# Pooled outputs of two batches issued by two engines, and a list scheduler that is told how long issuing a transfer takes

## The chip, the cores and the metric

The kernel runs on one core of one Trainium2 chip. The metric is the device time of one execution in microseconds (us). The kernel before has a median of 968.46 us over 3 runs (966.66 to 969.57).

The engines have these names here: TensorE (PE in the profile; its weight loads are PEld), VectorE (DVE), ScalarE (ACT), GpSimd (POOL) and SyncE (SP; SPq is its queue, which issues transfers). Each engine works through its own queue in order. An instruction that waits holds back all that stands behind it on the same engine.

## The reference

Attention with a pooled and a local part, followed by a token and channel mixer, for 8 batches of 8 heads, 576 positions and a head dimension of 64, all in float32:

```python
q_d, k_d, v_d = (means over 4 neighbouring positions: 144 positions)
out_d     = softmax(q_d @ k_d.T / 8) @ v_d
out_up    = np.repeat(out_d, 4, axis=2)
mask      = np.abs(pos[:, None] - pos[None, :]) < 4
out_local = softmax(where(mask, q @ k.T / 8, -1e9)) @ v
x  = (out_up + out_local), heads side by side: (8, 576, 512)
h  = relu(x^T @ w_tok1) @ w_tok2          # tokens 576 -> 256 -> 576
u  = x + h^T
h2 = relu(u @ w_ch1) @ w_ch2              # channels 512 -> 1536 -> 512
result = u + h2
```

## The kernel before

**Work of one batch.** Queries and keys arrive as four tiles `qk`, values twice: as `vr` (rearranged for pooling) and as `vw` (windows of rows for the local part). `pool_q` and `load_v` sum groups of four positions; for batch 0 the queries and keys are summed on VectorE, otherwise GpSimd does it. `pooled(st, two)` computes the pooled attention of one half of the heads: scores `sd`, exponentials `pd`, their transposes `td`, products `ad` with the pooled values `vd`, and the normalized output `od`. After the second half, the twelve blocks of `od` are copied by twelve transfers of 24 KB into the last rows of each window of `vw`. So the local part can add the pooled output: `local(st, t)` takes one of five tiles of positions, computes local scores `sc`, probabilities `P`, their transposes `pT`, and multiplies them with `vw` (`av`, line 576). The eight rows of `vw` that the pooled output fills are multiplied by a fixed pattern of ones, and the sum of both outputs comes from the same product. Its result is copied to `x` by ScalarE (line 581).

**Mixer.** `mix` splits `x` into two parts (`xh`), multiplies with W1 (`t`, then `hid`) and W2, adds `x`, and scales the result to two float16 parts (`uh`). `first` and `second` are the channel products (`c`, in two chunks of 256 and 320 positions, three float16 passes each); each of the twelve output tiles of `first` is split again by ScalarE and VectorE (`h`, lines 761 and 763).

**Weights.** They come as raw 64-bit words and are turned into float32 in the kernel: `to_f32` uses ScalarE (line 217), GpSimd (220, 223) and VectorE (228). W has nine pieces (five raw buffers), C1 and C2 have twelve tiles each (six raw buffers for C1; the raw tiles of C2 go into the buffers of `qk` and `vw` of batch 0, once these are read). All of this takes place beside batch 0.

**Order of the work.** The order of instructions on each engine is fixed when the program is built. For the start (batch 0 with all weights, and most of batch 1's attention and mixer) `drive` does it: a list scheduler over 71 streams, which are generators that yield steps. A step has an engine, a planned time, what it needs, and PSUM or SBUF slots that it takes and gives. `drive` takes the step that can start first by its own clocks; among steps of the same engine that could start within 0.15 us (`PATIENCE`) it takes the one whose stream stands first in `ORDER`:

```python
t = max([clock[e], it[2] if at is None else at] + [made[n] for n in needs] + ...)
...
best = min(some, key=lambda x: x[0])
best = max((x for x in some if x[0] <= best[0] + PATIENCE and x[1][1][0] == best[1][1][0]),
           key=lambda x: x[1][3])
```

Engine letters in steps are A ScalarE, G GpSimd, V VectorE, P TensorE, S SyncE. The streams are L (loads: 0 pooling of `qk`, 1 `vr`, 2 W, 3 `vw`, 4 C1, 5 C2), A and a (attention of batch 0 and 1: 0 and 1 pooled, 2 to 6 the local tiles), M and m (mixer of batch 0 and 1), U (what follows the channel products), W (conversion of W), S (scale of C1), C and D (conversion of C1 and C2), T (C2's second step), H and h (loads of batches 1 and 2), P and Q (channel products of batch 0). Where TensorE would wait before batch 0's first channel products, `keep_busy` puts products of a constant tile in (`busy`, line 157). What is left over when batch 0 is done, and batches 2 to 7, is woven between the channel products by a fixed rule that does not use `ORDER`.

The transfers of the pooled output and the planned time at which the windows are complete (`full`):

```python
yield step("S", 0.2, ("vw", b), ("od", b, 0), at=e)
for c, k, s, odd, par, jq in blocks():
    nc.sync.dma_start(st.vw[...], st.od[...])
make(("full", b), e, 3.0)
```

Of the kernel before, what the change touches and what calls it, by code (L numbers as in the profile page):

```python
# [20 lines left out]
WB = QB + 6  # L21
KB = 1 + WB + QB // 4
# [10 lines left out]
PATIENCE = 0.15  # L33


ORDER = ("P0 L2 T0 W0 D7 m1 L1 m0 C11 D11 C7 U1 P1 L5 W6 W5 W7 D5 L4 D2 C0 C6 C1 U0 A4 h0 C4 W3 M3 m3 D4 L3 M2 "
         "U2 A6 D10 S0 D9 a6 a0 C5 L0 A3 A2 M0 a1 C8 A1 D0 m2 a3 A5 W1 H0 M1 a5 W4 Q0 W8 D6 D8 a2 A0 D1 C9 W2 "
         "C2 C10 D3 C3 a4 ").split()


@with_exitstack
def tile_ups_attention_mixer(ctx, tc, qk, vw, vr, w1, w2, c1, c2, out):
# [87 lines left out]

    clock = dict(A=2.0, G=5.0, V=2.0, P=0.0, S=0.0, D=0.0)
    now = [0.0]
    free = {k: {i: 0.0 for i in range(n)} for k, n in SLOTS.items()}
    held = {}
# [2 lines left out]
    def step(engine, us, *needs, at=None, take="", give=""):  # L139
        return engine, us, needs, at, take.split(), give.split()  # L140

    def make(what, t, late=0.0):
        made[what] = (t or 0.0) + late
# [87 lines left out]
    def weight_loads(pieces, tag, name):  # L231
        raws = {}
        for i, (src, n) in enumerate(pieces):
            yield step("S", 0.1, *([(name, "read", i - BUFS[tag])] if i >= BUFS[tag] else []))
            raws[i] = T([src.shape[0], 2 * n], U32, tag, f"{name}{i}_raw")
            nc.sync.dma_start(raws[i], src)
            made[name, "raw", i] = fetched(src.shape[0] * n * 8)
            made[name, "raw"] = raws
# [87 lines left out]
    class Second(Channel):  # L326
# [22 lines left out]
        def loads(self):  # L349

            self.raws = made["C2", "raw"] = []
            for i in range(NF):
                if i < 4:
                    yield step("S", 0.1, *(("tile", 0, t) for t in range(len(TILES))))
                    t = T([128, S + KW], F32, "qk", f"C2_raw{i}")[:, :1024].bitcast(U32)
                else:
                    if i == 4:
                        yield step("S", 0.1, *(("av", 0, t) for t in range(len(TILES))))
                        four = T([128, 4, 1024], U32, "vw", "C2_raws")
                    elif i >= 8:  # L360
                        yield step("S", 0.1, ("C2", "read", i - 4))
                    t = four[:, i % 4]
                nc.sync.dma_start(t, u32(c2[i]))
                self.raws.append(t)
                made["C2", "raw", i] = fetched(2 ** 19)
# [28 lines left out]
    def load_v(st):  # L394
        st.vd = T([128, 3, 4, D + 1], F32, "vd", f"vd{st.b}")
        nc.gpsimd.memset(st.vd[:, :, :, D:D + 1], 4.0)
        ts, arrives = {}, {}

        def fetch(i):
            two, kc = divmod(i, 3)  # L400

            tag = "w" if st.b > 1 else "x" if st.b or i < BUFS["x"] else "xh"
            ts[i] = T([128, 4, 128], F32, tag, f"vr{st.b}_{i}")
            nc.sync.dma_start(ts[i], vr[st.b, kc, two].rearrange("p (r c) -> p r c", r=4))
            arrives[i] = fetched(262e3)

        early = {0: 6, 1: 5}.get(st.b, 0)
        if early:
            yield step("S", 0.1, *([("mixed", 0)] if st.b else []))
        for i in range(early):  # L410
            fetch(i)
        for i in range(6):
            two, kc = divmod(i, 3)
            if i >= early:
                fetch(i)
            t = ts.pop(i)
            e = yield step("G", 1.25, at=arrives[i])
            nc.gpsimd.tensor_add(t[:, 0:2], t[:, 0:2], t[:, 2:4])  # L418
            nc.gpsimd.tensor_add(st.vd[:, kc, 2 * two:2 * two + 2, :D], t[:, 0].rearrange("p (h d) -> p h d", d=D),
                                 t[:, 1].rearrange("p (h d) -> p h d", d=D))  # L420
            make(("v", st.b, i), e)
# [43 lines left out]
    def pooled(st, two):  # L465

        b = st.b
        yield step("P", 0.9, ("q", b, 2 * two + 1), take="gg")
        ps = P2(f"sd{b}_{two}")
        for c, k, s, odd, par, jq in blocks():  # L470
            x = st.qd[64 * par:64 * par + 64, 2 * two + odd]
            nc.tensor.matmul(ps[64 * c:64 * c + 64, k, Sd * s:Sd * s + Sd], x[:, QC * jq:QC * jq + 64], x[:, Sd:],  # L472
                             start=True, stop=True)
        mx = T([128, 2, 3], F32, "sm", f"mxd{b}_{two}")
        nm = T([128, 2, 3], F32, "nm", f"nmd{b}_{two}")
        s_ = ps[:, :, :3 * Sd].rearrange("p a (s w) -> p a s w", s=3)
        yield step("V", 1.25)
        nc.vector.tensor_reduce(mx, s_, axis=AX.X, op=ALU.max)
        nc.vector.tensor_scalar(nm, mx, -0.125 / 16, None, ALU.mult)
        yield step("A", 2.1, take="w", give="gg")  # L480
        pd = T([128, 2, 3, Sd], F32, "w", f"pd{b}_{two}")
        for k in range(2):
            for s in range(3):
                nc.scalar.activation(pd[:, k, s], s_[:, k, s], AF.Exp, bias=nm[:, k, s:s + 1], scale=0.125 / 16)  # L484
        yield step("P", 1.1, take="gg", give="w")
        ps = P2(f"td{b}_{two}")
        flat = pd.rearrange("p k s w -> p (k s w)")
        for kc in range(3):
            for c, k, s, _, par, _ in blocks():
                o, i = Sd * kc + QC * s, Sd * (3 * k + s) + QC * kc  # L490
                for i, n in [(i, 64)] if i + 64 <= 6 * Sd else [(i - 16, 64), (i, QC)]:
                    nc.tensor.matmul(ps[64 * par:64 * par + n, k, o:o + QC], flat[64 * c:64 * c + QC, i:i + n],  # L492
                                     ident[64 * c:64 * c + QC, 64 * c:64 * c + QC], start=True, stop=True)
        yield step("A", 0.95, take="w", give="gg")
        pt = T([128, 2, 3 * Sd], F32, "w", f"ptd{b}_{two}")
        nc.scalar.copy(pt[:64 + QC], ps[:64 + QC, :, :3 * Sd])
        yield step("P", 1.1, ("v", b, 3 * two + 2), take="gg", give="w")
        ps = P2(f"ad{b}_{two}")
        flat = pt.rearrange("p k n -> p (k n)")
        for t in range(3):  # L500
            for kc in range(3):
                for c, k, s, odd, par, _ in blocks():
                    if s == t:
                        o = 3 * Sd * k + Sd * kc + QC * s
                        n = min(64, 6 * Sd - o)
                        p = slice(64 * par, 64 * par + QC)
                        nc.tensor.matmul(ps[64 * c:64 * c + n, k, (D + 1) * s:(D + 1) * s + D + 1], flat[p, o:o + n],  # L507
                                         st.vd[p, kc, 2 * two + odd], start=kc == 0, stop=kc == 2)
        if not hasattr(st, "od"):
            st.od = T([128, 2, 3, 2, D], F32, "od", f"od{b}")  # L510
        ps = ps[:, :, :3 * (D + 1)].rearrange("p k (s w) -> p k s w", s=3)
        r = T([128, 2, 3], F32, "sm", f"rd{b}_{two}")
        e = yield step("V", 0.8, give="gg")
        nc.vector.tensor_scalar(r, ps[:, :, :, D], 4 * EPS, None, ALU.add)
        nc.vector.reciprocal(r, r)
        nc.vector.tensor_tensor(st.od[:, :, :, two], ps[:, :, :, :D], r.unsqueeze(3).to_broadcast([128, 2, 3, D]),
                                ALU.mult)
        make(("od", b, two), e)
        if two == 1:
            yield step("S", 0.2, ("vw", b), ("od", b, 0), at=e)  # L520
            for c, k, s, odd, par, jq in blocks():
                nc.sync.dma_start(st.vw[64 * par + 1 + WB:64 * par + KB, CG * jq:CG * jq + CG, 128 * odd:128 * odd + 128],  # L522
                                  st.od[64 * c:64 * c + QC, k, s].rearrange("p a d -> p (a d)"))
            make(("full", b), e, 3.0)
        make(("pair", b, two), e)

    def local(st, t):
# [38 lines left out]
        yield step("A", 0.59, give=one)  # L566
        nc.scalar.copy(pt, ps[:, :4 * n].rearrange("p (hp s) -> p hp s", hp=4))
        make(("tile", b, t), e)
        e = yield step("P", 0.8, ("full", b), ("vw", b), take="gg")
        ps = P2(f"av{b}_{t}")  # L570
        for hp in range(4):
            for j in range(nb):
# [144 lines left out]

    def ahead(b):

        yield step("S", 0.1, *([("C2", "read", i) for i in range(4)] + [("pair", 0, 1)] if b == 1 else []))  # L720
        st = load(b)
        if b > 1:
            load_w(st)
        yield from pool_all(st)
        yield from load_v(st)
        if b == 1:
            yield step("S", 0.1, *(("C2", "read", i) for i in range(4, NF)))
            load_w(st)

    def side(b):  # L730
# [94 lines left out]
        return mixes[b]  # L825

    def windows(st):
        yield step("S", 0.1)
        load_w(st)

    last = len(TILES) - 1
# [135 lines left out]
```

## Time and profile before

| what | value |
|---|---|
| median of 3 runs | 968.46 us (966.66 to 969.57) |
| the profiled execution | 967.55 us, of it 965.7 us from first to last instruction |
| mean TensorE clock granted | 0.975 |
| busy: TensorE, VectorE, ScalarE, GpSimd | 908.6, 431.0, 302.9, 202.6 us |
| constant products that keep TensorE busy (first 200 us) | 75, 24.8 us |
| moved by DMA | 71.67 MB |

Rows of a timeline give start and length in us, engine, line, operation, output from inputs, how many were merged; in brackets the idle time of that engine just before and what ended it. The forty digits of a slice row are busy tenths of 24 us each. In rows of stretches each engine's busy time is followed by its number of instructions. A row of the chain has start, length and the work that the end of the program was waiting for then.

### The profile page before, as it was taken

Reading aid. Unit: us, or ns where it says so; the run is one execution under the profiler, and the core shown is the slowest. Engines: PE = TensorE matmul, PEld = TensorE weight load, DVE = VectorE, ACT = ScalarE, POOL = GpSimd, SP = SyncE. Lnnn points to the kernel's source line nnn. Section 1 sums busy time; section 2 is a strip of 40 time slices with the busy share of each in tenths; the row PEclk is TensorE's granted clock in tenths of the full one; section 3 lists DMA queues with packets and bytes.
Section 4 is the critical chain, followed back from the end, with each engine's and each line's share of the span. In section 5 each row is a group of like instructions: output and inputs, shape, how many; then the busy total and the mean of one; then the engine's idle time right before and its main releaser. Section 6 shows DMA issues by size and latency. Waiting matters only on the chain.

```text
span 965.7 us, 29151 instructions
## 1 busy us (share of the span) xinstructions
PE 908.6 (94%) x13143; PEld 696.8 (72%) x13143; DVE 431.0 (45%) x982; ACT 302.9 (31%) x675; POOL 202.6 (21%) x301
## 2 busy tenths in 40 slices
PE   7658798999999999999999999999999999999998
PEld 3446576877867787777877787777777778777875
DVE  7539984526353354334353344324443254333221
ACT  2346463314242143223232142322332142322110
POOL 5659950042231002300122002300113000000000
PEclk8779799999999999999999999999999999999999
DMA  9561630251242012600243002500234000000000
GB/s 341 133 241 60 239 74 14 88 138 52 64 160 39 22 33 68 170 8 22 59 147 59 14 27 80 171 1 28 53 95 117 7 23 21 18 1 28 12 12 28
DMA packets 31756, 71.67 MB, mean 74 GB/s; under 512 B 3808, under 2 KB 16608, under 8 KB 31008
## 3 DMA queue, kind: packets, MB, share of 16 engines
q1 hardware_dynamic: 31632, 69.81, 24.0%
q8 instruction: 103, 1.69, 0.7%
q14 instruction: 21, 0.17, 0.1%
HBM read 58.00 MB, written 9.44 MB: 70 GB/s over the span
## 4 chain that ended last, share of the span: by engine, by line
PE 79%; DVE 10%; ACT 4%; issue 3%; SPq 1%; DMA 1%; POOL 0%; ACTq 0%; DVEq 0%
PE c L120 53%; PE t L120 11%; PE av L576 3%; PE ad L507 2%; PE td L492 2%; PE t L640 2%; PE pT L563 2%; PE sc L540 2%; DVE uh L686 1%; ACT pd L484 1%; SPq L522 1%; PE sd L472 1%; DVE P L552 1%; DVE r L557 1%; DVE mx L551 1%
## 5 line engine op out<-in xcount | busy, mean ns | idle before, releaser
L120 PE MATMUL c<-uh,CW 128*128 128x256 f16 (+1 forms) x2304 | 307.9, 288 | 0.4 <-DVE uh L686 0.4
L120 PE MATMUL c<-h,CX 128*128 128x256 f16 (+1 forms) x2304 | 306.2, 286 | 0.0
L120 PEld LDWEIGHTS <-CW 128*128 128x128 f16 x2304 | 218.2, 98 | 68.1 <-issue 12.2
L120 PEld LDWEIGHTS <-CX 128*128 128x128 f16 x2304 | 216.0, 98 | 60.6 <-issue 1.5
L763 DVE SCALAR_TENSOR_TENSOR h<-c,h 128x256 f16<-128x256 f32 (+1 forms) x192 | 87.7, 457 | 190.6 <-ACT h L761 190.4
L761 ACT ACTIVATE h<-c 128x256 f16<-128x256 f32 (+1 forms) x192 | 78.7, 410 | 237.9 <-PE c L120 237.6
L418 POOL TENSOR_TENSOR vr<-vr 128x256 f32<-128x256 f32 x48 | 36.9, 769 | 372.9 <-DMA vr<-in_vr_dram 350.2
L789 DVE SCALAR_TENSOR_TENSOR u<-c,io,u 128x256 f32<-128x256 f32 (+1 forms) x64 | 32.9, 514 | 104.3 <-PE c L120 104.2
L120 PE MATMUL t<-xh,W 128*128 128x512 f32 (+1 forms) x240 | 67.7, 418 | 0.3 <-ACT x L581 0.2
L120 PE MATMUL t<-W,hid 128*128 128x256 f32 (+1 forms) x384 | 66.9, 309 | 0.0
L443 POOL TENSOR_TENSOR qs<-qk 128x288 f32<-128x288 f32 x56 | 39.8, 711 | 125.5 <-DMA qk<-in_qk_dram 65.7
L665 ACT COPY u<-t 128x256 f32<-128x256 f32 (+1 forms) x64 | 25.4, 397 | 118.2 <-PE t L120 100.5
L667 DVE TENSOR_REDUCE umx<-t 128x1 f32<-128x256 f32 (+1 forms) x64 | 29.2, 456 | 67.0 <-ACT u L665 67.0
L618 DVE TENSOR_TENSOR xh<-x,xh 128x512 fp32r<-128x512 f32 (+1 forms) x40 | 30.9, 774 | 57.8 <-ACT xh L616 57.8
L576 PE MATMUL av<-vw,pt 47*32 47x64 f32 x2304 | 40.6, 230 | 15.6 <-DMA vw<-od 10.7
L120 PEld LDWEIGHTS t<-W,hid 128*128 128x128 f32 x384 | 53.0, 188 | 2.2
L120 PEld LDWEIGHTS t<-xh,W 128*128 128x128 f32 (+1 forms) x240 | 43.6, 193 | 11.4 <-issue 2.2
L576 PEld LDWEIGHTS av<-vw,pt 47*32 47x32 f32 x2304 | 29.3, 108 | 28.6 <-DMA vw<-od 12.6
L581 ACT COPY x<-av 128x512 f32<-128x512 f32 (+1 forms) x40 | 23.3, 583 | 68.3 <-PE av L576 59.9
L554 ACT ACTIVATE P<-P 128x304 f32<-128x304 f32 (+1 forms) x40 | 18.4, 459 | 67.8 <-DVE P L552 67.4
L684 ACT ACTIVATE uh<-u,us 128x256 f16<-128x256 f32 (+1 forms) x64 | 29.8, 524 | 28.4 <-DVE us L126 18.1
L686 DVE SCALAR_TENSOR_TENSOR uh<-u,us,uh 128x256 f16<-128x256 f32 (+1 forms) x64 | 34.0, 575 | 5.1 <-ACT uh L684 5.0
(107 smaller groups left out, 844.6 us busy)
## 6 DMA issues: line engine op xcount, KB each, us to landing
qk<-in_qk_dram SPq DMA_DIRECT2D x32, 579.0 KB
vr<-in_vr_dram SPq DMA_DIRECT2D x48, 256.0 KB
vw<-in_vw_dram SPq DMA_DIRECT2D x16, 702.0 KB
C_raw<-in_c_dram SPq DMA_DIRECT2D x16, 512.0 KB
out_dram<-u SPq DMA_DIRECT2D x32, 160.0 KB
C_raws<-in_c_dram SPq DMA_DIRECT2D x8, 512.0 KB
out_dram<-u SPq DMA_DIRECT2D x32, 128.0 KB
vw<-od SPq DMA_DIRECT2D x96, 24.0 KB
```

Of the source, the lines that this page charges most:

```text
L120: nc.tensor.matmul(ps, lhs(a), rhs(c), start=first and i == 0, stop=last and i == 2, **kw)
L418: nc.gpsimd.tensor_add(t[:, 0:2], t[:, 0:2], t[:, 2:4])
L443: nc.gpsimd.tensor_add(two, x[:, :, 0:2], x[:, :, 2:4])
L576: nc.tensor.matmul(ps[QB * j:QB * j + QB, par, D * hp:D * hp + D], pt[p, hp, QB * j:QB * j + QB], st.vw[p, g, D * COLUMN[hp]:D * COLUMN[hp ...
L618: nc.vector.tensor_tensor(xh[:, 1], xf(t), xh[:, 0].bitcast(F32), ALU.subtract)
L665: nc.scalar.copy(u, ps)
L667: nc.vector.tensor_reduce(umx[ch][:, c:c + 1], ps, axis=AX.X, op=ALU.max, apply_absolute_value=True)
L684: nc.scalar.activation(t[:, 0], st.u[ch][c], AF.Copy, scale=s)
L686: nc.vector.scalar_tensor_tensor(t[:, 1], st.u[ch][c], s, t[:, 0], ALU.mult, ALU.subtract)
L761: nc.scalar.activation(ht[:, 0], ps, AF.Relu)
L763: nc.vector.scalar_tensor_tensor(ht[:, 1], ps, 0.0, ht[:, 0], ALU.max, ALU.subtract)
L789: nc.vector.scalar_tensor_tensor(us[c], banks[c], io, us[c], ALU.mult, ALU.add)
```

## The change

The twelve transfers of the pooled output become two steps in batches 0 and 1: four are issued by ScalarE (planned 2.72 us) and eight by SyncE (planned 5.44 us), both at the time the output is ready; the windows are planned complete 2.0 us after SyncE's step instead of 3.0 us after the output. Other batches keep twelve on SyncE. Issuing a load is planned at 0.65 us instead of 0.1, each load of `vr` and of C2 has a step of its own, and SyncE's planned clock starts at 3.0. Some planned times of TensorE's steps grow (pooled attention from 0.9, 1.1, 1.1 to 1.1 in batches 0 and 1, 1.3, 1.3; the local products of batch 0 from 0.8 to 1.2). `ORDER` is a new permutation of the same 71 names. No arithmetic, tile or transfer is added or removed.

```diff
-ORDER = ("P0 L2 T0 W0 D7 m1 L1 m0 C11 D11 C7 U1 P1 L5 W6 W5 W7 D5 L4 D2 C0 C6 C1 U0 A4 h0 C4 W3 M3 m3 D4 L3 M2 "
-         "U2 A6 D10 S0 D9 a6 a0 C5 L0 A3 A2 M0 a1 C8 A1 D0 m2 a3 A5 W1 H0 M1 a5 W4 Q0 W8 D6 D8 a2 A0 D1 C9 W2 "
-         "C2 C10 D3 C3 a4 ").split()
+ORDER = ("h0 D4 M1 W6 U0 T0 D10 P1 C6 M3 C2 W5 C4 D2 D5 M2 W0 L2 m0 D11 C7 L0 a0 W4 S0 C10 D6 L5 m1 W3 W1 D7 "
+         "L1 a5 C5 A0 M0 A6 C8 A2 U2 A4 A1 L4 C1 C3 P0 C9 U1 m3 C11 m2 a6 W2 A5 a1 a4 D8 A3 D0 Q0 D1 H0 a3 W7 "
+         "D3 D9 W8 a2 L3 C0 ").split()
+ISSUE = 0.65
...
-    clock = dict(A=2.0, G=5.0, V=2.0, P=0.0, S=0.0, D=0.0)
+    clock = dict(A=2.0, G=5.0, V=2.0, P=0.0, S=3.0, D=0.0)
...  (weight_loads)
-            yield step("S", 0.1, *([(name, "read", i - BUFS[tag])] if i >= BUFS[tag] else []))
+            yield step("S", ISSUE, *([(name, "read", i - BUFS[tag])] if i >= BUFS[tag] else []))
...  (C2.loads)
                 if i < 4:
-                    yield step("S", 0.1, *(("tile", 0, t) for t in range(len(TILES))))
+                    yield step("S", ISSUE, *(("tile", 0, t) for t in range(len(TILES))))
                     t = T([128, S + KW], F32, "qk", f"C2_raw{i}")[:, :1024].bitcast(U32)
                 else:
+                    yield step("S", ISSUE, *((("av", 0, t) for t in range(len(TILES))) if i < 8 else [("C2", "read", i - 4)]))
                     if i == 4:
-                        yield step("S", 0.1, *(("av", 0, t) for t in range(len(TILES))))
                         four = T([128, 4, 1024], U32, "vw", "C2_raws")
-                    elif i >= 8:
-                        yield step("S", 0.1, ("C2", "read", i - 4))
...  (load_v)
-        if early:
-            yield step("S", 0.1, *([("mixed", 0)] if st.b else []))
         for i in range(early):
+            yield step("S", ISSUE, *([("mixed", 0)] if st.b and i == 0 else []))
             fetch(i)
...  (pooled)
-        yield step("P", 0.9, ("q", b, 2 * two + 1), take="gg")
+        yield step("P", 0.9 if b > 1 else 1.1, ("q", b, 2 * two + 1), take="gg")
...
-        yield step("P", 1.1, take="gg", give="w")
+        yield step("P", 1.3, take="gg", give="w")
...
-        yield step("P", 1.1, ("v", b, 3 * two + 2), take="gg", give="w")
+        yield step("P", 1.3, ("v", b, 3 * two + 2), take="gg", give="w")
...
         if two == 1:
-            yield step("S", 0.2, ("vw", b), ("od", b, 0), at=e)
-            for c, k, s, odd, par, jq in blocks():
-                nc.sync.dma_start(st.vw[...], st.od[...])
-            make(("full", b), e, 3.0)
+            ready_at = e
+            for engine, share in ((("A", (0, 4)), ("S", (4, 12))) if b < 2 else (("S", (0, 12)),)):
+                e = yield step(engine, 0.68 * (share[1] - share[0]) if b < 2 else 0.2, ("vw", b), ("od", b, 0), at=ready_at)
+                for c, k, s, odd, par, jq in list(blocks())[share[0]:share[1]]:
+                    rows = st.vw[...]
+                    (nc.scalar if engine == "A" else nc.sync).dma_start(rows, st.od[...])
+            make(("full", b), e, 2.0 if b < 2 else 3.0)
...  (local)
-        e = yield step("P", 0.8, ("full", b), ("vw", b), take="gg")
+        e = yield step("P", 0.8 if b else 1.2, ("full", b), ("vw", b), take="gg")
...  (ahead, windows)
-        yield step("S", 0.1, *([("C2", "read", i) for i in range(4)] + [("pair", 0, 1)] if b == 1 else []))
+        yield step("S", 4 * ISSUE if b == 1 else 0.1, *([("C2", "read", i) for i in range(4)] + [("pair", 0, 1)] if b == 1 else []))
...
-            yield step("S", 0.1, *(("C2", "read", i) for i in range(4, NF)))
+            yield step("S", 2 * ISSUE, *(("C2", "read", i) for i in range(4, NF)))
...
-        yield step("S", 0.1)
+        yield step("S", 2 * ISSUE)
```

More of the change, by code (lines that the diff above doesn't have):

```diff
@@ L519, in pooled @@
         if two == 1:
-            yield step("S", 0.2, ("vw", b), ("od", b, 0), at=e)
-            for c, k, s, odd, par, jq in blocks():
-                nc.sync.dma_start(st.vw[64 * par + 1 + WB:64 * par + KB, CG * jq:CG * jq + CG, 128 * odd:128 * odd + 128],
-                                  st.od[64 * c:64 * c + QC, k, s].rearrange("p a d -> p (a d)"))
-            make(("full", b), e, 3.0)
+            ready_at = e
+            for engine, share in ((("A", (0, 4)), ("S", (4, 12))) if b < 2 else (("S", (0, 12)),)):
+                e = yield step(engine, 0.68 * (share[1] - share[0]) if b < 2 else 0.2, ("vw", b), ("od", b, 0), at=ready_at)
+                for c, k, s, odd, par, jq in list(blocks())[share[0]:share[1]]:
+                    rows = st.vw[64 * par + 1 + WB:64 * par + KB, CG * jq:CG * jq + CG, 128 * odd:128 * odd + 128]
+                    (nc.scalar if engine == "A" else nc.sync).dma_start(rows, st.od[64 * c:64 * c + QC, k, s].rearrange("p a d -> p (a d)"))
+            make(("full", b), e, 2.0 if b < 2 else 3.0)
         make(("pair", b, two), e)
```

## The prediction

> **What bounds the kernel now.** I read the page first: the span, the forty slices, the DMA queues.
>
> ```profile
> span 965.7 us, 29151 instructions
> PE   7658798999999999999999999999999999999998
> DVE  7539984526353354334353344324443254333221
> POOL 5659950042231002300122002300113000000000
> PEclk8779799999999999999999999999999999999999
> DMA  9561630251242012600243002500234000000000
> q8 instruction: 103, 1.69, 0.7%
> ```
>
> The reader is to see two kernels in one. From slice 10 (about 240 us) on, TensorE is at 9 in nearly every slice at full clock. Before that it has holes, its clock drops, and VectorE and GpSimd stand at 9 in slices 3 and 4. The table of importance and the changed costs mostly work in that first part, so I cut the span into five stretches, and two of them finer:
>
> ```profile
> core 0: us, PE busy (x) PEld busy (x) DVE busy (x) ACT busy (x) POOL busy (x), PEclk, DMA share, GB/s
> 0.00:110.00 110.00, 76.31 (x1194) 49.69 (x1195) 76.92 (x155) 46.24 (x98) 77.54 (x94) 0.82 0.57 188
> 110.00:150.00 40.00, 40.00 (x610) 32.04 (x610) 31.93 (x71) 23.08 (x51) 23.76 (x34) 0.95 0.48 140
> 150.00:170.00 20.00, 16.37 (x259) 11.49 (x256) 9.68 (x21) 6.89 (x14) 0.00 (x0) 0.91 0.07 16
> 170.00:240.00 70.00, 67.75 (x970) 53.24 (x969) 32.56 (x73) 21.89 (x52) 17.23 (x29) 1.00 0.33 96
> 240.00:965.70 725.70, 708.19 (x10119) 550.33 (x10116) 279.89 (x664) 204.80 (x463) 84.03 (x145) 1.00 0.18 53
> 41.00:58.00 17.00, 9.95 (x243) 6.14 (x235) 4.83 (x12) 2.14 (x5) 0.18 (x1) 0.70 0.20 53
> 60.00:118.00 58.00, 43.68 (x410) 31.81 (x408) 50.50 (x87) 32.27 (x63) 53.70 (x48) 0.85 0.52 192
> ```
>
> Columns: length, then busy time of TensorE, weight load, VectorE, ScalarE, GpSimd, clock, DMA share. TensorE lacks 110.00 - 76.31 = 33.69 us in the first 110 us, nothing to 150, 20.00 - 16.37 = 3.63 around 160, 70.00 - 67.75 = 2.25 to 240. After 240 it is 708.19 / 725.70 = 98% busy with work that the change does not touch; whatever is won or lost before simply shifts it. From 60 to 118 us GpSimd is busy 53.70 of 58.00 us and VectorE 50.50: this stretch is paced by converting the weights. But from 41 to 58 us GpSimd works 0.18 of 17.00 us and VectorE 4.83. That hole is where the change acts; the timelines of the engines and the chain show what fills it:
>
> ```profile
> 46.36 0.56 DVE L516 TENSOR_TENSOR od<-ad,rd 128x384 f32<-128x384 f32 x1
> 46.95 8.67 SPq L522 DMA_DIRECT2D vw<-od  x12
> 54.24 2.17 DMA vw<-od
> 54.31 0.44 PE L576 MATMUL av<-vw,pt 47*32 47x64 f32 x8 [2.56 <-DMA vw<-od]
> 56.45 1.75 PE L576 MATMUL av<-vw,pt 47*32 47x64 f32 x102 [1.01 <-DMA vw<-od]
> 42.76 0.74 ACT L246 CAST W<-W_raw 128x256 fp32r<-128x256 f32 x2
> 57.37 0.59 ACT L581 COPY x<-av 128x512 f32<-128x512 f32 x1 [13.88 <-PE av L576]
> 57.85 0.67 ACT L217 ACTIVATE C_raw<-C_raw 128x512 f32<-128x512 f32 x1
> 58.68 1.35 POOL L223 TENSOR_SCALAR C_raw<-C_raw 128x512 bf16<-128x512 f32 x1 [17.50 <-ACT C_raw L217]
> 55.66 1.49 SPq L236 DMA_DIRECT2D W_raw<-in_w_dram  x2
> ```
>
> The pooled output of batch 0 is written at 46.36 + 0.56 = 46.92. SyncE then issues its twelve transfers one after another for 8.67 us, the last lands 2.17 us after its issue began, and the local `av` products, which read these rows, run in drips until 56.45. ScalarE's next instruction is the copy of `x` (13.88 us waiting on `av`), and behind it in its queue stands the conversion of a C1 tile, for which GpSimd waits 17.50 us. Two more weight loads stand on SyncE behind the twelve. One issue train thus stops five engines. Batch 1 repeats it with TensorE better covered:
>
> ```profile
> 152.60 8.56 SPq L522 DMA_DIRECT2D vw<-od  x12
> 159.85 0.32 PE L576 MATMUL av<-vw,pt 47*32 47x64 f32 x8 [2.10 <-DMA vw<-od]
> 160.57 0.30 PE L576 MATMUL av<-vw,pt 47*32 47x64 f32 x2 [0.41 <-DMA vw<-od]
> 161.98 0.76 PE L576 MATMUL av<-vw,pt 47*32 47x64 f32 x38 [1.11 <-DMA vw<-od]
> 162.68 3.21 PE L120 MATMUL c<-uh,CW 128*128 128x320 f16 x12
> 167.03 1.79 PE L120 MATMUL c<-uh,CW 128*128 128x320 f16 x12
> ```
>
> 8.56 us of issues, and TensorE idle 2.10 + 0.41 + 1.11 = 3.62 us of the 3.63 that the stretch lacks.
>
> **The change part by part.** Durations are from the profiled execution, 967.55 us (span 965.7 and 1.85 around it); the median of the runs shown is 968.46, 0.91 above it.
>
> *The split, batch 0.* No transfer is added; four of twelve move from SyncE to ScalarE, in the first two batches only.
>
> ```profile
> L522 SPq DMA_DIRECT2D vw<-od x96: 668/669/1573, 46.9 to 812.9; - x96
> ```
>
> One issue is 0.669 us, 8.67 / 12 = 0.72 with the gap. Eight in a row end the train four issues sooner: 4 x 0.72 = 2.9 us, the four of ScalarE running beside them. I take -2.9. Bounds: 0, if ScalarE comes to its four so late that its last lands no sooner than now, and -2.9, since SyncE still has eight. What queues behind them: SyncE's weight loads (at 55.66) move up as much; on ScalarE four issues cost 4 x 0.669 = 2.7 us (no row shows ScalarE issuing; I use SyncE's median, its ends 0.668 and 1.573 give 2.7 to 6.3), which lie in a stretch where ScalarE is busy 2.14 of 17 us. The DMA engines are nearly empty there, share 0.20 in the stretch from 41 to 58. [...]
>
> *The new costs around the store, batch 0.* The planner had the pooled rows ready 3.0 us after the output is written; the profile has 56.45 - 46.92 = 9.5 us. After the change it plans 8 x 0.68 + 2.0 = 7.44 us against 8 x 0.72 + 2.17 = 7.9 us to expect. It sees 7.44 - 3.0 = 4.4 us more of wait, and fills queues with what can start earlier: the C1 conversion at 57.85 should stand ahead of the copy at 57.37 and GpSimd resume sooner. The lower bound is 0 (nothing is moved ahead, or the copy stays first); the upper is the idle 17.50 us less the 2.9 already counted, 14.6, because GpSimd at 53.70 of 58.00 passes an earlier start on nearly whole. I take half of the 4.4, -2.2, nearer the lower end, since VectorE paces the same stretch and its chain begins with that `x`, which does not move by this.
>
> *The split, batch 1.* SyncE's train from 152.60 ends four issues sooner, 4 x 8.56 / 12 = 2.9 us of the 3.62 idle. There is a second term: right after the wait, twelve 128x320 matmuls take 3.21 us where the same twelve take 1.79 at 167.03, and the stretch's clock is 0.91. With some 0.8 us of idle left I expect full clock, 1.4 us more. The nearest row that a shorter wait keeps the clock is the stretch from 170 to 240: 2.25 us idle in pieces, clock 1.00. [...] Sum -4.3, bounds 0 and -(3.6 + 1.4) = -5.0 as gain; as loss ScalarE's 2.7 us of issuing stand in front of `h` and `CX` work, of which SyncE's place shows nothing: at most +2.7 if the products wait for it. ScalarE is idle half of that time, so I add 0.
>
> *Separate steps for transfers, 0.65 us each, and SyncE's clock starting at 3.0.* No instruction is added. The six `vr` loads, now one block, will interleave with weight loads:
>
> ```profile
> 3.44 4.95 SPq L404 DMA_DIRECT2D vr<-in_vr_dram  x6
> 21.84 0.64 POOL L419 TENSOR_TENSOR vd<-vr 128x128 f32<-128x128 f32 x1
> 30.49 0.33 PE L507 MATMUL ad<-vd,ptd 48*64 48x65 f32 x4 [0.66 <-ACT ptd L496]
> 36.41 2.22 PE L507 MATMUL ad<-vd,ptd 48*64 48x65 f32 x68 [5.59 <-issue]
> 32.66 0.66 ACT L217 ACTIVATE C_raw<-C_raw 128x512 f32<-128x512 f32 x1
> 34.00:36.00 2.00, 0.00 (x0) 0.00 (x0) 0.00 (x0) 0.00 (x0) 1.84 (x3) 0.50 0.87 323
> ```
>
> The last `vr` is issued by 3.44 + 4.95 = 8.4 us. With up to eight loads between the six, at the 0.72 us of the train above, it is some 5 us later. Its sum on GpSimd ends at 22.5 now and its first user is at 30.49: 8 us of cover, cost 0; without the cover at most 5 us, and the gain of weights that come sooner at most the same. The sixth to eighth C2 load become steps of their own, and the loads of batch 1 (2.6 us where it was 0.1) and of `vw` (1.3) are costed: the order on SyncE may change, no transfer is added, and what they feed (C2, batch 1) is read tens of microseconds later, cost 0.
>
> *Larger costs of pooled products and first `av`; the new table.* Only the order of each engine's queue changes. The table decides among steps of one engine that can start within 0.15 us, so nearly always where an engine is behind. What that is worth no row shows. Bounds by the nearest: the 5.59 us gap at 36.41 (TensorE waits for nothing shown, VectorE and ScalarE run dry behind it) may vanish or come twice, so -5.6 to +5.6. I take 0.
>
> Sum: -2.9 - 2.2 - 4.3 = -9.4, so 967.55 - 9.4 = 958.2, and 0.9 up for the median: 959.1 us.
>
> **The rivals.** *Conversions refill the hole.* If the planner puts two thirds of the 17.50 us of GpSimd's idle to use, 11.7 + 4.3 = 16.0 us go: 952.5. For it: GpSimd at 93% afterwards. Against: VectorE at 87% and products waiting for `x`.
>
> *ScalarE is held, slower.* ScalarE's four issues wait in its queue for the pooled output. Its last conversion before that ends at 43.50, 3.4 us ahead of the output. If the new order puts the issues ahead of conversions and something like the 5.59 us gap delays the output, GpSimd starves behind ScalarE as it now does behind `x`, but earlier, and batch 1's `h` can be caught the same way. Each microsecond goes to the end at 93%; from 9.4 + 2.9 = 12.3 us of extra hold it decides. Measured from the last ScalarE work before the gap, 32.66 + 0.66 = 33.3, to 46.92 the hold is 13.6 us: 968.46 - 9.4 + 13.6 = 972.7.
>
> *The gain is given back.* Batch 1's own chain ends just in time now:
>
> ```profile
> 228.48 0.38 PE L120 MATMUL c<-uh,CW 128*128 128x256 f16 x2 [0.41 <-DVE uh L686]
> 231.88 2.08 DVE uh L686 x3
> ```
>
> TensorE goes from the last products of batch 0 to the first of batch 1 with 0.41 us idle, the scaled inputs (`uh`) finished as they are read. If batch 0 ends 9 us sooner and the chain of batch 1 does not (its tiles `a1`, `a2`, `a3` fall from places 46, 62, 51 to 56, 69, 64 of 71), TensorE waits there and 7 to 9.4 us of the gain return: 966 to 968.5, middle 967. Against it: TensorE is full from 110 to 150, so batch 1's steps wait for TensorE and move with it. A code-loading wait would act alike: the page's instruction row has 103 transfers, and the 5.59 us gap, in which nothing but GpSimd works, falls where the DMA engines are busy at 0.87; one more such gap takes 5.6 of the 9.4 (964.7, still the forecast), two take it all.
>
> **How the numbers follow.** 0.3%, about what a measurement here can tell from no change, is 2.9 us: 965.6 to 971.4. Forecast (953 to 965) 0.50; refill 0.14; given back 0.17; held 0.19. The first two are faster, 0.64; the third the same, 0.17; the last slower, 0.19. The range for eight in ten takes the first three, from 948 (batch 0 at 14.6 + 2.9 and batch 1 at 4.3 would be 946.7; most of it is enough) to 972.
>
> **What would show it.** Right: SyncE with eight transfers in about 5.7 us after the output of batch 0 and four on ScalarE beside them; `av` finished starting about 7.9 us after the output; GpSimd's idle of 17.50 us cut to 12 or less; the wait before `av` of batch 1 under 1 us and no twelve at 3.21 us; the same 725 us from the place that is now 240 on. Wrong: ScalarE's issues late or ahead of conversions that GpSimd waits for; a new idle piece of TensorE over 3 us at the change from batch 0 to 1; the 5.59 us gap larger or doubled.

## The result, and the profile after

The changed kernel takes 956.8 us in the median of 4 runs (950.54 to 957.6); the kernel before, beside it, 967.56 us (965.69 to 969.57). The ratio is 0.9874, 95% interval 0.9827 to 0.9922: 10.8 us, or 1.3%, faster. A second series gave 0.9878 (0.9851 to 0.9904). The profiled execution took 957.6 us, its span is 955.6.

The page of the changed kernel:

```profile
span 955.6 us, 29167 instructions
PE   7568999999999999999999999999999999999998
PEclk8877799999999999999999999999999999999999
q10 hardware_dynamic: 448, 0.20, 0.1%
```

q10, ScalarE's transfer queue, is new: 448 packets, 0.20 MB, the stores that moved. TensorE still has its holes in the first slices and is at 9 after that. The stretches (length, then busy time of TensorE, weight load, VectorE, ScalarE, GpSimd, clock, DMA share):

```profile
0.00:110.00 110.00, 80.70 (x1194) 51.61 (x1195) 77.27 (x161) 47.25 (x99) 78.43 (x95) 0.77 0.58 190
110.00:150.00 40.00, 40.00 (x556) 32.03 (x554) 30.41 (x66) 22.82 (x52) 23.66 (x33) 0.98 0.45 135
150.00:170.00 20.00, 20.00 (x496) 16.21 (x494) 13.07 (x32) 6.29 (x12) 0.00 (x0) 1.00 0.11 30
170.00:240.00 70.00, 68.10 (x985) 53.59 (x983) 30.70 (x68) 24.48 (x57) 17.12 (x30) 1.00 0.32 96
```

TensorE is busy for 20.00 of 20.00 us from 150 to 170, where it had been for 16.37: the wait in batch 1 is gone, and the clock there is 1.00 instead of 0.91. Until 110 us it is busy 4.4 us longer, but the clock is 0.77 instead of 0.82. To place the gain I cut each span at two events: TensorE's first channel product of batch 0 ("first c") and of batch 1 ("seam"). Of the kernel before, then of the changed one:

```profile
110.37 2.76 PE L120 MATMUL c<-uh,CW 128*128 128x256 f16 x12
226.81 1.26 PE L120 MATMUL c<-uh,CW 128*128 128x256 f16 x10
```

```profile
108.57 2.77 PE L121 MATMUL c<-uh,CW 128*128 128x256 f16 x12
219.28 1.75 PE L121 MATMUL c<-uh,CW 128*128 128x256 f16 x12
```

| | first c | first c to seam | seam to end |
|---|---|---|---|
| before (span 965.7) | 110.37 | 116.44 | 738.9 |
| changed (955.6) | 108.57 | 110.71 | 736.3 |
| difference | -1.8 | -5.7 | -2.6 |
| predicted | -5.1 | -4.3 | 0 |

These are single executions; a second one of the changed kernel has 107.85 and 218.40, so differences of under 1 us say nothing. The last 2.6 us I ascribe to nothing: a version below with the very TensorE queue of the kernel before measured 736.1 there.

Batch 0's stores in the changed kernel, from the timelines of VectorE, ScalarE's and SyncE's queues, GpSimd and TensorE, and one row of SyncE's waits (waiting line, what for: us in all, times, longest):

```profile
41.31 0.56 DVE L514 TENSOR_TENSOR od<-ad,rd 128x384 f32<-128x384 f32 x1
41.90 3.41 ACTq L523 DMA_DIRECT2D vw<-od  x4
44.30 2.44 SPq L237 DMA_DIRECT2D W_raw<-in_w_dram  x4
46.83 6.01 SPq L523 DMA_DIRECT2D vw<-od  x8
SPq L237 <- DMA vw<-od: 13.9, 2, 13.2
45.36 0.66 ACT L218 ACTIVATE C_raw<-C_raw 128x512 f32<-128x512 f32 x1 [6.24 <-DVE CW L229]
46.17 1.34 POOL L224 TENSOR_SCALAR C_raw<-C_raw 128x512 bf16<-128x512 f32 x1 [12.71 <-ACT C_raw L218]
51.53 0.97 PE L576 MATMUL av<-vw,pt 47*32 47x64 f32 x48 [2.56 <-DMA vw<-od]
```

The output is written at 41.87, 5 us earlier than before (in the version below with this plan and no split, at 44.36). ScalarE issues its four at once. SyncE does not: it stands 13.2 us at a weight load until the first of ScalarE's stores has landed, then issues four loads, the second as ScalarE's second store lands, and only then its eight, at 46.83, 5 us after the output. `av` resumes at 51.53, 9.7 us after the output (before: 56.45 - 46.92 = 9.5).

### The profile page after: what moved, and what is told of

It reads as the page before. It is cut to its first block, busy times and chain, and to the rows that moved or that the text cites. A ratio compares the mean times of both kernels' runs of the same rounds, so it can differ in the third digit from the quotient of the medians.

```text
span 955.6 us, 29167 instructions
## 1 busy us (share of the span) xinstructions
PE 910.0 (95%) x13141; PEld 697.2 (73%) x13141; DVE 427.1 (45%) x982; ACT 301.9 (32%) x675; POOL 203.1 (21%) x301
## 4 chain that ended last, share of the span: by engine, by line
PE 79%; DVE 9%; ACT 3%; issue 3%; DMA 2%; POOL 2%; SPq 1%; ACTq 0%; POOLq 0%; DVEq 0%
PE c L121 51%; PE t L121 12%; PE av L576 3%; PE td L490 2%; PE t L640 2%; PE ad L505 2%; PE sc L540 2%; PE pT L563 2%; ACT pd L482 1%; DVE uh L686 1%; SPq L523 1%; DVE r L557 1%; PE busy L158 1%; DVE P L559 1%; DMA vr<-in_vr_dram 1%
## 5 line engine op out<-in xcount | busy, mean ns | idle before, releaser
L121 PE MATMUL t<-xh,W 128*128 128x512 f32 (+1 forms) x240 | 70.2, 426 | 0.6 <-DVE xh L618 0.6
L121 PE MATMUL t<-W,hid 128*128 128x256 f32 (+1 forms) x384 | 70.6, 319 | 0.0
L121 PEld LDWEIGHTS t<-W,hid 128*128 128x128 f32 x384 | 55.3, 195 | 3.4 <-DVE hid L654 1.1
L576 PE MATMUL av<-vw,pt 47*32 47x64 f32 x2304 | 38.4, 228 | 5.2 <-DMA vw<-od 3.3
```

What stands on the lines that cost most here:

```text
L121: nc.tensor.matmul(ps, lhs(a), rhs(c), start=first and i == 0, stop=last and i == 2, **kw)
L576: nc.tensor.matmul(ps[QB * j:QB * j + QB, par, D * hp:D * hp + D], pt[p, hp, QB * j:QB * j + QB], st.vw[p, g, D * COLUMN[hp]:D * COLUMN[hp ...
```

## The experiments

Each comparison is with the kernel before in the same series (its median there: 965.27 for the first four, 967.57 for the second four, 965.48 for the last three). First c and seam are from the profiled executions.

| version | median, us | ratio, 95% interval | first c | seam |
|---|---|---|---|---|
| split alone | 962.58 | 0.9964 [0.9943, 0.9985] | 111.22 | 224.09 |
| changed, no split | 954.7 | 0.9898 [0.9878, 0.9918] | 107.95 | 219.14 |
| changed, old table | 955.61 | 0.9899 [0.9865, 0.9933] | 105.81 | 222.33 |
| new table alone | 973.66 | 1.0095 [1.0059, 1.0131] | 129.67 | 234.44 |
| changed, again | 956.1 | 0.9878 [0.9851, 0.9904] | 107.85 | 218.40 |
| all costs alone | 958.38 | 0.9910 [0.9891, 0.9929] | 97.52 | 221.68 |
| store's cost alone | 965.91 | 0.9982 [0.9962, 1.0002] | 98.40 | 225.87 |
| loads' costs alone | 962.31 | 0.9948 [0.9930, 0.9967] | 109.63 | 222.87 |
| products' costs alone | 958.8 | 0.9920 [0.9892, 0.9947] | 111.41 | 223.02 |
| changed, W's last loads behind the stores | 987.41 | 1.0215 [1.0181, 1.0249] | 152.68 | 251.11 |
| changed, no split, C1's loads late | 977.25 | 1.0111 [1.0077, 1.0145] | 102.29 | 242.93 |

**The split alone.** The kernel before with the four stores on ScalarE, and nothing else moved in any queue:

```diff
-                nc.sync.dma_start(st.vw[...], st.od[...])
+                (nc.scalar if b < 2 and s == 0 else nc.sync).dma_start(st.vw[...], st.od[...])
```

> The kernel before with one edit: four of the twelve pooled-output transfers are issued by ScalarE in batches 0 and 1. Plan, costs and table stay, so every other queue is the same instruction for instruction. Split theory (the terms of the prediction): -2.9 us in batch 0, -4.3 in batch 1, so 7 us less than before, with the wait before av in batch 1 under 1 us. Planner theory (the new costs and the new order move other work into the holes, the split does little): 0 to 3 us less than before.

2.7 us are gained, which lies in the planner theory's range. Its timelines of ScalarE's and SyncE's queues, of ScalarE and of TensorE, batch 0 and then batch 1, and one stretch:

```profile
46.80 3.39 ACTq L522 DMA_DIRECT2D vw<-od  x4
49.13 0.33 SPq L236 DMA_DIRECT2D W_raw<-in_w_dram  x1
50.34 6.19 SPq L522 DMA_DIRECT2D vw<-od  x8
154.17 5.77 SPq L522 DMA_DIRECT2D vw<-od  x8
157.34 0.44 ACT L761 ACTIVATE h<-c 128x320 f16<-128x320 f32 x1 [4.11 <-DMA vw<-od]
158.35 1.79 PE L120 MATMUL c<-uh,CW 128*128 128x320 f16 x12 [1.05 <-DVE h L763]
160.78 0.64 PE L576 MATMUL av<-vw,pt 47*32 47x64 f32 x38 [0.27 <-DMA vw<-od]
150.00:170.00 20.00, 18.68 (x413) 14.16 (x408) 11.32 (x25) 8.31 (x16) 0.00 (x0) 1.00 0.09 25
```

In batch 0 SyncE's eight end at 50.34 + 6.19 = 56.53, later than all twelve had (46.95 + 8.67 = 55.62), and first c does not come sooner. In batch 1 they end at 159.94 instead of 161.16, although the output is written 1.6 us later there; `av`'s waits shrink from 3.62 us to 0.27, TensorE's idle time from 150 to 170 from 3.63 to 1.32, the clock stays at 1.00, and the way from first c to seam is 112.87 instead of 116.44. Not all of the shorter wait is won: ScalarE stands 4.11 us until its stores are out, `h` comes late, and TensorE waits 1.05 us for it. So the split earns its gain in batch 1 alone.

**The changed kernel without the split.** All twelve on SyncE, with the queues of TensorE, VectorE and GpSimd as in the changed kernel:

```diff
-                    (nc.scalar if engine == "A" else nc.sync).dma_start(rows, ...)
+                    nc.sync.dma_start(rows, ...)
```

> The changed kernel with all twelve transfers issued by SyncE at the same places of the plan; TensorE, VectorE and GpSimd keep their queues instruction for instruction. Split theory: 7 us more than the changed kernel, 964. Planner theory: within 2 us of the changed kernel, 955 to 959, because in batch 1 TensorE has other products until 168.4 us (twelve issues from 157.3 would land at 157.3 + 12 x 0.72 + 2.2 = 168.1), and in batch 0 SyncE's eight start at 46.83 although the output is written at 41.87: W loads ahead of them wait for ScalarE's transfers, and without that wait twelve from 41.9 end at 50.5, sooner than eight from 46.83 (52.8).

```profile
44.38 8.68 SPq L523 DMA_DIRECT2D vw<-od  x12
157.12 8.95 SPq L523 DMA_DIRECT2D vw<-od  x12
150.00:170.00 20.00, 20.00 (x495) 16.24 (x493) 12.86 (x31) 6.36 (x12) 0.00 (x0) 1.00 0.11 30
```

It is as fast as the changed kernel as far as these runs tell (0.9898 against 0.9874 and 0.9878, the intervals overlap), as the planner theory said, and the simpler of the two. SyncE's twelve end at 44.38 + 8.68 = 53.06, the eight of the split version at 46.83 + 6.01 = 52.84. Measured from the output the twelve end sooner: 8.7 us after it (44.36) against 11.0 (41.87). In batch 1 the train takes 8.95 us and TensorE is still busy 20.00 of 20.00: the plan has channel products there, and the first `av` starts only at 168.

**The two tables.** The changed kernel with the old `ORDER`, and the kernel before with the new `ORDER` alone:

```diff
-ORDER = ("h0 D4 M1 W6 U0 T0 D10 P1 C6 ...
+ORDER = ("P0 L2 T0 W0 D7 m1 L1 m0 C11 ...
```

> The changed kernel with the old table of importance; costs and split stay. If the costs carry the gain: within 3 us of the changed kernel, 954 to 960. If the table carries it: 964 or more.

> The kernel before with the new table of importance alone, with the old costs and no split. If the costs carry the gain: no better than the kernel before, 966 or more, since the planner still takes the pooled rows for ready 3 us after the output. If the table carries it: 955 to 961.

With the new costs the table makes no difference that these runs tell (0.9899 and 0.9878, the intervals overlap). Without them it costs 8.4 us: first c comes 19.3 us later, at 129.67, and 7.6 us of that delay reach the seam. The new table belongs to the new costs; alone it is a loss.

**The changed kernel again, and the costs one by one.** The costs alone: the changed kernel with the old table and one step of twelve stores on SyncE, planned 8.16 us. The store's cost alone, in the kernel before:

```diff
-            yield step("S", 0.2, ("vw", b), ("od", b, 0), at=e)
+            e = yield step("S", 0.68 * 12 if b < 2 else 0.2, ("vw", b), ("od", b, 0), at=e)
...
-            make(("full", b), e, 3.0)
+            make(("full", b), e, 2.0 if b < 2 else 3.0)
```

The loads' costs alone are the hunks with `ISSUE` and SyncE's clock at 3.0; the products' costs alone are the four raised planned times of TensorE's steps.

> The changed kernel once more, beside the three below on the same chip. All theories: a ratio of 0.985 to 0.992.

> The kernel before with all the new planned costs (loads 0.65 us each, SyncE's clock from 3.0, larger TensorE steps, the twelve pooled transfers as one SyncE step of 8.16 us and the windows complete 2.0 us behind it), the old table and no split. If the costs carry the whole gain: as good as the changed kernel, ratio 0.985 to 0.993. If split and table each bring a part that the other replaces: 0.994 or more.

> The kernel before with the store's cost alone: a step of 8.16 us on SyncE and the windows planned complete 10.2 us after the output instead of 3.0, batches 0 and 1. The theory of the store (the planner fills the wait behind the pooled output): most of the gain, ratio 0.988 to 0.994, and GpSimd's idle of 17.5 us well under 12. The theory of the loads (the initial order of transfers matters): 0.997 or more.

> The kernel before with the loads' costs alone: 0.65 us for each load, vr loads as steps of their own, SyncE's clock from 3.0; the store stays at 0.2 and 3.0, TensorE's steps as before. The theory of the loads: ratio 0.988 to 0.994. The theory of the store: within 0.3% of the kernel before, or above.

> The kernel before with the larger planned costs of TensorE's pooled products and of the first `av` product alone. Of the planned costs the loads' gave a ratio of 0.9948 and the store's 0.9982, and all together 0.991; the products of the two ratios is 0.993. Theory one: the costs add up, so these give what is left, a ratio of about 0.998 (2 us less). Theory two: they are worth more together than one by one, and these alone give nothing or a loss: 0.999 to 1.005. A ratio of 0.995 or less would make them a source of the gain by themselves.

The costs alone, without split and table, give 0.9910: most of the gain. The products' costs, from which neither theory expected more than 2 us, are a source by themselves; the loads' 0.9948 lies between the ranges of the two theories on them. One by one the three give 0.9982, 0.9948 and 0.9920, whose product, 0.985, is more than they give together. Why they don't add up is shown only in part. The products' and the loads' costs each shorten the wait in batch 1: TensorE's busy time from 150 to 170 us is 19.37 and 18.13, before 16.37. The store's cost lengthens it, alone and with the others. Alone it cuts GpSimd's idle piece from 17.50 to 3.60 us and brings first c 12 us sooner (98.40), which is the rival of the refilled hole and not the 2.2 us of the forecast; then it gives this back, the other rival's story. Two of its stretches, and the second of them with all costs together:

```profile
110.00:150.00 40.00, 37.37 (x654) 29.21 (x654) 24.56 (x54) 17.90 (x42) 20.25 (x31) 1.00 0.38 103
150.00:170.00 20.00, 12.89 (x469) 9.85 (x461) 17.47 (x39) 10.71 (x18) 0.00 (x0) 0.83 0.25 81
```

```profile
150.00:170.00 20.00, 14.46 (x433) 10.51 (x428) 15.76 (x32) 11.70 (x21) 4.33 (x7) 0.74 0.38 135
```

With the store's cost alone, 2.63 and 7.11 us of idle and a clock of 0.83 stand where batch 1 now waits, for its own stores among others, and the seam comes only 0.9 us sooner. With all costs 5.54 us of idle and a clock of 0.74 stand there.

**W's last loads behind the stores.** The changed kernel, with SyncE free when the output is written. Meant as a version that beats both:

```diff
+            make(("issued", b), e)
...
-            yield step("S", ISSUE, *([(name, "read", i - BUFS[tag])] if i >= BUFS[tag] else []))
+            yield step("S", ISSUE, *([(name, "read", i - BUFS[tag])] + ([("issued", 0)] if name == "W" else []) if i >= BUFS[tag] else []))
```

> The changed kernel, with the last four weight loads of W planned behind the issues of the stores of batch 0, so that SyncE can issue its eight stores when the output is written and not some 5 us later (41.9 against 46.8 us). Theory one: the stores' landing sets the first `av`; `av` starts up to 5 us sooner and the kernel takes 952 to 955 us, the fastest so far. Theory two: the gain at the first `c` is given back at the first product of batch 1, as it was when the store's cost alone was changed, or the later weight loads cost as much: 956 us, no difference from the changed kernel.

Both theories fall: it is the slowest of all. Its queues of ScalarE and SyncE, SyncE's waits, and first c on TensorE:

```profile
43.15 3.40 ACTq L523 DMA_DIRECT2D vw<-od  x4
45.51 6.09 SPq L523 DMA_DIRECT2D vw<-od  x8
SPq L523 <- DMA vw<-od: 14.0, 2, 13.6
152.68 1.48 PE L121 MATMUL c<-uh,CW 128*128 128x256 f16 x12
```

It does answer another question. No load stands ahead of the eight now, and they still start only 2.36 us after ScalarE's four. Over four kernels, SyncE's next transfer starts 2.40 (changed), 2.29 (old table), 2.33 (split alone) and 2.36 us after ScalarE's first store in batch 0. SyncE's longest wait that a landing of `vw<-od` ends is 13.2, 6.3, 13.5 and 13.6 us there. So in batch 0 it is not the weight loads that delay SyncE but ScalarE's stores. Why first c is 44 us late I did not follow to its end; GpSimd pools queries and keys of batch 1 from 108.72 us on, ahead of the last conversions of C2 (120.72) and of W (122.15).

**C1's loads late.** The version without the split, with C1's loads 2 to 5 planned behind W's last one, to see whether fewer bytes in flight shorten TensorE's waits for nothing shown:

```diff
-... if i >= BUFS[tag] else []))
+... if i >= BUFS[tag] else [("W", "raw", 8)] if name == "C1" and i > 1 else []))
```

> The changed kernel with all twelve stores on SyncE (954.7 us) and with the third to sixth load of C1 planned behind the last load of W, so that fewer bytes are moved in the first 35 us. Theory one: TensorE's waits for nothing shown (some 13 us in the first 45 us) are transfers of its own instructions that queue behind loads; with fewer loads in flight they shrink by several us, and the first `c` comes sooner by part of it, if the conversions of C1 aren't late in their turn. Theory two: they have another cause and stay at 10 to 13 us; the time is the same or longer.

```profile
29.06 0.71 PE L505 MATMUL ad<-vd,ptd 48*64 48x65 f32 x15 [5.43 <-issue]
53.45 0.64 POOL L221 TENSOR_SCALAR C_raw<-C_raw 128x512 uint32<-128x512 uint32 x1 [8.10 <-DMA C_raw<-in_c_dram]
```

Inconclusive for its question: the waits over 0.6 us sum to 9.8 us instead of 12.6 in the changed kernel, the largest is still 5.43, and GpSimd starves 8.10 us for C1. First c comes at 102.29 and the seam at 242.93, another early start that batch 1 does not follow.

**Blocks of instructions.** A program that does none of the reference's computation:

```python
small(ps[0], x, 2048)                       # matmuls of 64x32 by 64x38, each with its weight load
for i, t in enumerate(big): nc.sync.dma_start(t, src[i % 18])   # 24 loads of 0.5 MB
small(ps[1], y, 2048)
```

> A measurement by itself, which leaves out the whole computation: 2048 small matmuls, each with its weight load, run with no transfer in flight, then 2048 more while SyncE's queue loads 24 blocks of 0.5 MB. Theory one: TensorE's instructions come in blocks of 16,384 bytes, and a block's transfer is late when the DMA engines are full: the first half has no pauses of over 0.3 us, the second has one of 1 to 5 us at every 128th pair. Theory two: the pauses don't hang on the load of the DMA engines: both halves have them alike, or neither has.

SyncE's loads wait for nothing that the first half makes, so they ran beside it and not beside the second. The trace counts two products for each call (8192 for 4096). Timeline of TensorE, and two stretches (length, TensorE, weight load, VectorE, GpSimd, clock, DMA share, GB/s):

```profile
14.11 2.25 PE L29 MATMUL ps<-x 64*32 64x38 f32 x128 [4.50 <-issue]
70.25 2.25 PE L29 MATMUL ps<-x 64*32 64x38 f32 x128 [1.48 <-issue]
0.00:40.00 40.00, 17.25 (x991) 16.21 (x992) 1.48 (x26) 0.20 (x4) 1.00 0.81 317
40.00:127.00 87.00, 54.06 (x3081) 50.47 (x3084) 0.00 (x0) 0.00 (x0) 1.00 0.02 5
```

Every 128 products with their weight loads, 256 instructions, TensorE pauses: 3.95 to 4.50 us from 14 to 33 us, while the loads run, and 1.21 to 1.76 us from 40 us on, without them. Each theory holds by half: the pauses are there anyway, and while the loads run (DMA share 0.81 in the first 40 us, 0.02 behind them) they are about three times as long.

## Why the prediction was right, and where it was not

The total came out, 956.8 us against 959.1, but in good part by luck. Of the 9.4 us forecast, 7.2 were the split's and 2.2 the planned costs'. The split alone gave 2.7, and beside the new costs none that these runs tell (0.9874 and 0.9878 against 0.9898 with the new table, 0.9899 against 0.9910 with the old). The planned costs alone gave 9.2.

*The split, batch 0 (-2.9): failed.* It assumed that SyncE's eight start at the output, beside ScalarE's four. SyncE waits for ScalarE's stores to land (13.2 us at the weight load), so its eight end at 52.84, where the twelve of the version without the split end at 53.06, from an output 2.5 us later. The split alone shows it directly: 56.53 against 55.62. The trace of the changed kernel names the semaphore on which each transfer reports its landing: eight numbers (101 and 103 to 109) for the 289 transfers of both queues. In batch 0 SyncE's first load has 105, the semaphore of ScalarE's first store: the store has landed at 44.21, SyncE's wait for 105 stands at 44.23, and the load is issued at 44.30. It is the same with the second load and ScalarE's second store, both on 106: landed at 45.39, wait at 45.41, issued at 45.46. In batch 1 SyncE's first store has 108 and ScalarE's first 107, and they start side by side (157.32 and 157.37). No run gave the queues semaphores of their own, so what the split would gain in batch 0 without the sharing is not shown. (The landing of 2.17 us that the forecast used is that of the eleventh transfer, issued at 54.24, not of the last.)

*The new costs around the store (-2.2): the mechanism was right, its size and its passing on were not.* ScalarE's conversion at 45.36 stands ahead of the copy of `x`, as foretold, and GpSimd's idle piece fell to 12.71 us. By 60 us GpSimd has done 4 us more work, by 90 us 4.85. Of the kernel before and of the changed one (TensorE, weight load, VectorE, ScalarE, GpSimd, clock):

```profile
0.00:60.00 60.00, 40.63 (x846) 24.47 (x847) 33.64 (x83) 17.59 (x41) 31.20 (x55) 0.77 0.68 207
60.00:90.00 30.00, 22.37 (x276) 16.42 (x273) 24.13 (x40) 19.76 (x39) 27.54 (x25) 0.89 0.54 208
90.00:110.00 20.00, 13.30 (x75) 8.79 (x76) 19.15 (x33) 8.89 (x20) 18.81 (x16) 0.85 0.31 99
```

```profile
0.00:60.00 60.00, 40.98 (x925) 25.74 (x925) 39.34 (x91) 22.39 (x53) 35.35 (x58) 0.83 0.70 217
60.00:90.00 30.00, 23.12 (x208) 15.34 (x206) 24.36 (x38) 17.32 (x34) 28.24 (x23) 0.77 0.49 189
90.00:110.00 20.00, 16.60 (x64) 10.52 (x64) 13.58 (x33) 7.55 (x15) 14.84 (x15) 0.61 0.37 108
```

GpSimd's lead is then lost between 90 and 110, where GpSimd is busy 14.84 instead of 18.81 us and TensorE's clock is 0.61. The timeline of the changed kernel's TensorE shows a part of how:

```profile
88.39 0.61 PE L640 MATMUL t<-ident,x 128*128 128x128 f32 x3 [2.00 <-DVE umx L667]
88.93 1.15 PE L121 MATMUL t<-W,hid 128*128 128x320 f32 x6
90.95 0.48 PE L333 MATMUL C_sum<-CX 128*128 128x128 bf16 x4 [0.88 <-DVE CX L229]
92.09 1.97 PE L121 MATMUL t<-W,hid 128*128 128x320 f32 x6
99.20 1.97 PE L121 MATMUL t<-W,hid 128*128 128x320 f32 x6
```

Behind an idle piece of 2.00 us and one of 0.88 the clock, 1.00 from 86 to 91 us, is 0.57 from 91 to 92 and 0.50 from 92 to 102, and three groups of products with W2 on the path to first c take 1.97 instead of 1.15 us, 2.5 us in all; before, the four such groups all took 1.14 to 1.16. Three groups of 1.97 us stand in the second execution of the changed kernel and in the one without the split too. TensorE's own lead was smaller by then: it is 4.9 us where `av` resumes (51.53 for 56.45) and already down to 2.4 at the first of these groups (88.93 for 91.33). From 60 to 90 us its clock is 0.77 instead of 0.89; more of that part I did not follow. The forecast let an earlier start of GpSimd pass on "nearly whole" in its upper bound; TensorE's clock was left out.

*The split, batch 1 (-4.3): size right, cause shared.* The split alone gains 3.6 us from first c to seam, where 2.9 of wait and 1.4 of clock were foretold: on that way TensorE is idle 2.46 us instead of 3.63, and its 1649 products take 110.41 us instead of 112.81, at a clock of 0.99 instead of 0.97. In the changed kernel the new plan removes the same wait by itself, since the version without the split has it gone too. ScalarE is held, but at no cost; its timeline and TensorE's:

```profile
157.37 3.11 ACTq L523 DMA_DIRECT2D vw<-od  x4
160.53 0.44 ACT L761 ACTIVATE h<-c 128x320 f16<-128x320 f32 x1 [4.15 <-DMA vw<-od]
168.42 0.86 PE L576 MATMUL av<-vw,pt 47*32 47x64 f32 x64
```

`h` waits 4.15 us for the stores, more than the 2.7 us allowed for, and TensorE does not notice; in the split alone it lost 1.05 us by it.

*Loads' costs (0) and products' costs with the table (0, bounds -5.6 to +5.6): undersized.* Alone, the loads' costs measured -5.3 us, the products' -6.7 and the table +8.4, each of the latter outside the bounds, which were for the two together; that pair was not run. I had taken re-ordering to be worth nothing because no row priced it.

*The rivals.* "Conversions refill the hole" and "given back" are both real: with the store's cost alone 12 us at first c shrink to 0.9 at the seam. The prediction had whatever is won before simply shift the rest; there it does not. In the changed kernel nothing was given back, TensorE being busy 40.00 of 40.00 and 20.00 of 20.00 us ahead of the seam. "ScalarE is held" costs nothing there. The signs named for a right forecast came half true: `av` starts again 9.7 us after the output, not 7.9, GpSimd's idle piece is 12.71, and the wait in batch 1 is gone.

## What to carry to other kernels

Splitting an issue train over two queues was worth here only what the wait at its end was worth (3.6 us from first c to seam, with the split alone), and a list scheduler that is told the true cost can fill that wait with other work; with both, the split gained nothing more here. Look at the first transfer behind the train on the other queue, and at the semaphore that the trace names for it: in batch 0 of the changed kernel it was that of the train's first store, and the transfer was issued 0.09 us after that store had landed (44.30 for 44.21); in batch 1 it was another, and both were issued side by side. Judge a change of a plan at the last event that the rest hangs on (here the first product of batch 1), for a start that is 12 us sooner may arrive there as 0.9.

## What the runs showed of the hardware

TensorE's waits for nothing shown recur by the count of its products in the program of blocks, every 128 of them, and nearly so in the changed kernel. In its timeline:

```profile
14.24 1.39 PE L490 MATMUL td<-ident,pd 48*64 48x48 f32 x76 [2.02 <-issue]
18.38 0.70 PE L540 MATMUL sc<-qk 64*32 64x38 f32 x36 [2.08 <-issue]
29.40 0.49 PE L505 MATMUL ad<-vd,ptd 48*64 48x65 f32 x15 [4.72 <-issue]
```

They sum with the next two (2.68 and 1.09) to 12.6 us in the first 45, the DMA share of the first 40 being 0.80. The last three come 127 or 128 products with weight loads after the one before, the second 105 after the first; transfers of 16,384 bytes on the instruction queue (q8) begin 2.4 to 2.8 us before the end of each but the first, for which the trace shows none. In the program of blocks the count between two pauses is 128 products with their weight loads, 256 instructions, and a pause is 1.21 to 1.76 us without other transfers and 3.95 to 4.50 beside the loads. The prediction bounded the new order by one such gap that goes or comes twice; in the first 45 us the waits for nothing shown sum to 5.78 us in the kernel before (0.19 and 5.59, ahead of the 224th and the 479th product; one of 3.03 ahead of the 119th is put down to ScalarE) and to 12.6 in the changed kernel (ahead of the 119th, 224th, 351st, 479th and 606th). What part of that the order brings no run shows.
